# A written-out TensorE order that also names banks and sets, with residual loads moved and zero matmuls in more places

## The chip, the core and the metric

The kernel runs on one core of one Trainium2 chip. The metric is the time on the device in microseconds, from the core's start to its end. Times of several runs are given as their median and their spread; the profile is of one further execution.

## The reference

The input is x, 2048 tokens of 640 numbers. After a layer norm two branches read it, and their outputs are added to x. The first is attention with 32 query heads of 20 numbers that share one key head and one value head; the second is a feed-forward layer of width 1728 with SiLU. All inputs are bf16.

```python
xn = layernorm(x)                                   # 2048 x 640, eps 1e-5
q = (xn @ wq) -> 32 heads x 2048 x 20 ; k = xn @ wk ; v = xn @ wv   # k, v: 2048 x 20
p = softmax(q @ k.T * 20 ** -0.5)                    # per head, 2048 x 2048
attention = concat_heads(p @ v) @ wo
ffn = silu(xn @ w1) @ w2                             # w1: 640 x 1728, w2: 1728 x 640
return x + attention + ffn
```

## The kernel before

**One planner, five written orders.** The file is a program that plans the kernel. `Sched` and `Builder` keep a clock for every engine and a duration for every operation, place the operations one by one at planned times, and write each engine's instructions in the order so found, with semaphores between engines. On the chip there is no choice left: every engine, and SP's queue of DMAs too, works in its written order, and a planned time has no force except through the order that came out of it.

**Tiles.** The work of attention is 2048 blocks: 4 query chunks of 512 tokens, 32 heads, 16 key tiles of 128 tokens. Four heads that follow each other make a group; there are 32 groups of 64 blocks. A head has 20 numbers, so a head's queries and keys stand in a strip of 32 partitions, and four scores of different strips run beside each other in the array: block number modulo 4 is the strip, the "row". A score is one matmul (32x128 weights, 512 columns) into one PSUM bank of 128x512 (L1010, in the first part L1421).

**From scores to sums.** A score's exponential is made in one of two ways. ScalarE reads one, two or three neighbouring banks at once and writes the exponentials into slots of a ring of 30 (L1034, before that L1444). Or VectorE clamps the score to an integer whose bits are the exponential (L1050, L1461), and VectorE or GpSimd add two offsets to three such blocks at once (L1489, L1495), which gives three pieces that are summed with three scalings of the values. A "set of sums" is up to four matmuls side by side in four strips of 32 columns, one for each head of the group, which add one piece each to the group's sums in bank 7 (`UBANK`; L1092, in the first part L1336). When a group is complete, VectorE copies the sums out (L1539), a DMA on SP's queue transposes them (L1508), VectorE takes the reciprocal of the denominators (L1522) and GpSimd scales (L1527). Banks 0 to 6 serve scores and all other matmuls.

**Jobs.** The query projections of later chunks and the feed-forward and output products are cut into jobs of 4 to 19 steps. A step is four matmuls of 32 columns beside each other (L569), 512 or 320 wide. The last step of a job may instead be cut into four row pieces (L1188), which run beside scores in a strip that is free. A query job ends with a copy out of its bank (L1640) and small DMAs that bring heads to their strips (L1649). Residual rows of x are loaded again for the outputs (`load_res`, L1826), 8 loads of 160 KB for the last and the first chunk, and are read first by L1767.

**Modes.** Scores and row pieces use the array by rows; sums and job steps use it by columns. Going from one to the other costs PE time, which the planner knows as `SWITCH`.

**The order around the change.** The first part (normalisation, keys, values, first queries, first scores) is planned greedily by `step`; in its gaps `fill` puts zero matmuls (L1252), so that PE is not idle. When at least 64 blocks are scored and the first part's jobs are used up, `step` enters the string `ORDER`, one letter for each PE step:

- a and A: a score for ScalarE; the capital closes the group of banks that one exponential reads.
- d and D: a score for VectorE; the case tells which engine adds the first offset.
- p: a set of sums. j: a job step. k: a row piece of a job step.

In the kernel before, the letters say what comes next but not where: `run_banks` and `one_bank` choose banks by the planned times at which they come free, and `open_pv` takes for each head the first piece that is ready at the planned time. `tail` does what is left after the string.

**SP's queue.** SP takes the DMA that is ready first in planned time. The eight residual loads may not be placed before the planned time `RES_AT`:

```python
if op.name == "res":
    op.at = RES_AT
```

Of the kernel before, what the change touches and what calls it, by code (L numbers as in the profile page):

```python
# [14 lines left out]
P = 128  # L15
# [35 lines left out]
RES_AT = 62.0  # L51
# [33 lines left out]
    "aADDaAdppdaAppaAaAppppaADdDppaAdppaADjjdaAkppDaAkpjdaAkppjadkApjaAkppppaADDjpppDaAkjaADkpjpadkAjjjpa"  # L85
    "ADjpjaADppDaAdppDaAjjaADjjdaApjDaAppjjjaADjjpaAdppaADpjjpaADpjaAdjjDaAppDaADppaAdppdaAdppaAdjpaAdjja"
    "ADjjaAdpppjaADkpppaAdkjjdaAkpjdakApppaADjjjdaAjjjaADkjpdaAkpjdaAkjpdakAjjjjjAAdppDaApppDaAdpppaDAppD"
    "aAdjjaAppdadAjjjaDAppaAdjjpjdaApjjaAdpppDaAppDaADpjjaADpjaADpjaAdpjDaAjjjjpjaAdppaADjjjjjaADppAAdppp"
    "aAdppDaADjjjaADppaADpjjaAdpaAdppjjdaAjjpaAdpjdaAppDaADppaADjpjadAkjjpDaAkjjjjadAkjpjakADjjjdaAjjjjaD"
    "AkjjjDaAkjjjDaAkjjjDakApppaAdppDaAjpDaAkjjdaAkjpDaAkppDkaApppaDAppDDaAppdaAppDaApppdaAappDDAppdaAjjp"  # L90
    "aADkjjpaDAkjjjDaAkjpjdakAjjjjaDAppdaAppADaAppjjjADDAkjjjjaAdkjpdaAkjjjjaDAkjpDaAppdaApppadAdpppDaApp"
    "aDdApDaApppADAkppadAkjjaAdkjjpakADppdaAppaAdppDDAAppdaAjjjjpaADkjjjdAAkjpjaADkjjjjaAdkppDDAAppdaAjpj"
    "aADkjpjDaAkjjpjaAdkjpjdakAjpDaAjjjdaApppdaAdppDaAppaADppDaADppADAppjDaAkjpaADkpjjaADkppakAkjjjdaAkpj"
    "jdaAkjjjjaAdkjjjjaDAppaDAppDaADppDaApppadAppaADDppDaAppdaAkjjjjaAdkjjjjDaAkjjkAdAppjDaApjpDaApjpAAdp"
    "dAAdpjppaADjaADjjjaADppDAApjDaAjjaAdpjjpdaAppaADpppdaAppdaAdpppaDAppaADpDdaApjjaAdjjjadApaAdppppDaAD"
    "pjjaADpjaADpjjaADppaDAjjjdaAjpjpaAdjjjjjaDAppdaApppdaAdppaADjjaAdjpjjpaADaADpppjjaAdpjadApjjdaAjpjjd"
    "aApdaApppdaAdjjpaAdpaAdppppdaAjjjaAdDjjpaDApadApjjjDaAjpjaADpppDaAkpjDaAkjpjdaAkpdakAppjaAdpDadAppDa"
    "AjjpdaAjDaAjpjDadAppjaAppjaAddjjjadApppAADppDdaApjjpaAdjdaAjjpDaApjpaAdjjaAdpjjaAdppaADpppDDaApjjpaA"
    "dkjjjaAdkjjjdaAkjjjjaAkDjpdaAjjjjjDaApDdaApppaAdppDAAppDaADpppaAdpdAAdpjjaADpjaADpjaADjpdaAppDaAjpjj"
    "aADkjjjaAakjjjjAddkjjjkaAjjjDaAjjpaAdppaAddppdaApppaAdDppaAdppaAdppdaADpppaAdppaADDppaADpDaApjpaDAjj"  # L100
    "jdaAkjjjdaAkjjjjjaADkjjjDakAjjjDaAppdaAppjaAaAjjjjpaDAdppdaAppaADDpppADAppadAdppadApppadAappDADppDaA"
    "pjjjaADjjjaDAjpAAdkjjjjdaAkjjjjaAdkjjjDkaApppAaaAppaADpjpjjjjjDaDAjjjjjjAADkjjadAkppjdAAkjpjjAkADppD"
    "AAdppaAdppadDApppaDdAppdaAppDaAdppaAkppdaAkppDaAkjjDaAkjjpaADdppaAdpjjaADkjjjaADkjjjjaADkjpDaAkjpjDa"
    "AkjjjDaApjpdaAkppDakApjpaAdppakAppDDaAppDaApppDaAdpjaAjjjjaAaAjjjjjjjjjaADdjjppdaAjpDaAjpjDaAppdDaAp"
    "paADppjaADkjjjjaAdkjjpaAdkjpkdaAjpjjdaAkjpjDaAkjjjaAdkjpdaAkpppdaADppaAdppDaApdaADpppaADDppaAppaADDp"
    "pDaAjjaADpjaADjpjjaAdjjjjpaADaAjpppjDaAdjjjpaAdpaAdpppDaAdpppDaApdaADppaAdppDaApjjDaAjjaAdjpaADjppja"
    "AdjjpjpaADaAjjjppdadAjpjpaADpdaApjpjadAjpDaAjjdaAjpjjaAdjpjaDAppjpDaAjjDaAppjadADjpppaDAaAjjpjpdaAdj"
    "jpaADpaAdpppdaAdpjpadAjjadAjjadAppadAdppDaAjppaAdjdaAjjjaADdppaAjjjjAADdpjpjaAjjAADpjjaDAppaAdppdadA"
    "pppaDAppDaAppAAdDpjjaAdjaDAjppaDADjpppaAdaDAppjjaAdppaAdjjjpaAdjpaAkjppdaAkjjdaAkppdaAkjjjjaAkjjjjaA"
    "dkjjjaAdkjjjkdaAjjjjaAdppDdaApppDaAppdaADppaAdppdaAppdaADpppaADppDaAkjjjaAdkjjjadAjjjjakAjjjdaAdjjjj"  # L110
    "jaAdpkdaAppdaDAppadApppdaAdpjaAkpjadAkjDaAkpppDaAkpjdaAppaADdppDaAppdaAppDaAjppaDAjjjDaAkjpjDaAkpjjj"
    "aAdkjjjkdaAjppaADkppaADkjpjdaAkpjjdaAkppDaADppDaAjjjjDaAkppaAdkjjjdaAkpjpDakAppDaAkppDaAkppjDaAkppaA"
    "DkjppdaAkpjDaAkppDAAkjjpkdAAjjjppdAAkppAAkjpaAddjpppdakAjaAdpjdkaAjjjjjaADkjjpaAkjjjAADdjpjpjAAkdjjj"
    "daAppkaADjjppdaADppDaAppAADdppaADjjjjaADkjjjjaADkjjpaAdkjpDkaApjjjaAdpjdaAjjpjaAdppdaADppaAdppaADDpp"
    "aAdjjjjaADkjpjaADkpjDaAkpjjjkDaAjjDaAkpjjpDaAkppdaAkppaAdkpjpadAkppdaAkppaAdppDADkpkAaAjppADAdjjjpja"
    "ADkjjaAdkjjjjjaADkjjjdkaAjjjjaADppdaAdppaADppAAdpppaADaAdpjjjjaAdjppaAdppaADjpjjDaAjjpDaApdAApppddaA"
    "pppDaAdppAAdppAADpDaApjjjaADdpjjppaAdpDaApjjjaAdjjdaAjjpjDaAjjdaApjjjpdaAjjdaApjjjjdaApjDAppAdaAjjpj"
    "jjdaAdpjjjjjjDaAjjjjaAdpppDaAppddaAppAADppdaAdppDaApppAAdDppaADjppdaAjjaAdjjdaAjjpjDaAjppdaAjpdaAjpj"
    "jjjDaApppdaApDaADppAADpjjjjjaADkjdaAkjjjjjaAddjjpjjaADkjjDkaAppjaADppdaAdppDaAppaAdppDaADpppaADppaAD"
    "pjjaAdjjjdaAkjjdaAkjjjjDaAkjjjjdAkAjjjDaAppdaApjjpaAaAjjjjjjjjjDaAdjjjjjjaADkppdaAkppAADkppjdkaAppaA"  # L120
    "DppdaAappAddpppaAapppAaADpDdpppDaAdppaADjjjjaAdjjaADkppdaAkjjjDaAkjjjjkDaAjjpjDaAjjpDaAppdaADppaADpp"
    "AADppaAdapppADppAAdDpjjjaADkjjjaAdkjjaAdkjjjjjkaAAAjjjjpjpdadApppAdAdppaAdppDaADppaAdjjjjaAdkjjjjadA"
    "kjpjaDAkjjdakAppppaADkpaAdkpppDdAAkpjjppjAkADaADpjpjjpjjjpjjjpjDaAjjjpjjAADApjjjjdADAjpjjjpjjjpjjjaA"
    "ADaApjjjjjpjjjpjjjjpjjjjjppjjpjjpjjjpjjjpp"
)
Z_COST = 0
# [351 lines left out]
class Builder:  # L478
# [97 lines left out]
    def steps_init(self):  # L576
# [26 lines left out]
        self.jl = []  # L603
        self.tq = [[[] for _ in range(4)] for _ in range(self.NG)]
# [364 lines left out]
    def open_score(self, tok, now):  # L969
# [9 lines left out]
        if act and self.grp is None:  # L979
            n = 0  # L980
            for t in ORDER[self.at:]:
                n += t in "aA"
                if t == "A":
                    break
            r, run, bt = self.run_banks(n, now)
            if run is None:
                return INF
            first = min(run, key=lambda b: (bt[b] > now + 1e-9, b))
            if bt[first] > now + 1e-9:
                return bt[first]  # L990
            if self.blk_pos + n > NBLK:
                self.blk_pos = 0
            self.grp = {"banks": run, "todo": list(run), "b0": self.blk_pos, "at": nb}
            self.blk_pos += n
        if act:
            todo = self.grp["todo"]
            bt = {b: self.bank_at(b) for b in todo}
            b = min(todo, key=lambda b: (max(bt[b], now + 1e-9), b))
            if bt[b] > now + 1e-9:
                return bt[b]  # L1000
            todo.remove(b)
        else:
            r, b = self.one_bank(now)
            if r > now + 1e-9:
                return r
# [54 lines left out]
    def open_pv(self, now):  # L1060
# [7 lines left out]
        for q in self.tq[g]:  # L1068
            got, when = None, INF
            for it in q[:8]:  # L1070
                r = max(sc.ready(it), self.reads_ready([("vv", it.kt // 2)]))
                if r <= now + 1e-9:
                    got = it
                    break
# [3 lines left out]
            elif not (closed and len(q) < most):  # L1078
                return when
# [1205 lines left out]
```

## Time and profile before

| | |
|---|---|
| median of 3 runs | 682.20 us |
| the runs | 682.20, 682.48, 679.81 us |
| the profiled execution | 679.33 us |
| its span, first to last instruction | 677.2 us |
| mean granted TensorE clock | 0.995 |
| PE, ACT, DVE, POOL busy | 98%, 96%, 93%, 83% |
| score matmuls in the order, in the first part | 1977, 71 |

Busy time is the time in which an engine had at least one instruction in work; matmuls overlap, and their ends are modelled, so PE's share alone does not say how much of it is needed. In the timeline a row gives the start, the length, the engine, the line, the operation and its shapes, how many instructions were merged into it, and in brackets the idle time before it with what ended it. A mean length of one instruction contains its latency; the spacing of the starts is the price.

### The profile page before, as it was taken

To read this page: it belongs to the slowest core of one execution; us is meant where nothing else is said; L and a number is where in the kernel's file an instruction comes from. 1 tells how busy PE (TensorE), PEld (TensorE's weight loads), DVE (VectorE), ACT (ScalarE), POOL (GpSimd) and SP (SyncE) were. 2 spreads that over 40 slices of the span, in tenths; PEclk is the share of its full clock that TensorE was granted. 3 is DMA by queue.
4 is the path that set the end of the run, shared out by engine and by line. 5 is a ranking of instruction groups with operands and counts; after the bars stand their busy time and mean duration, and the time that the engine had idled before them with its cause. 6 is when DMAs were issued, how large, how long until landed. Compare 5 with 4: busy or idle time off the path is not lost.

```text
span 677.2 us, 22217 instructions
## 1 busy us (share of the span) xinstructions
PE 666.5 (98%) x9690; PEld 226.9 (34%) x9693; DVE 632.8 (93%) x1136; ACT 652.6 (96%) x798; POOL 561.6 (83%) x443
## 2 busy tenths in 40 slices
PE   9799999999999999999999999999999999999997
PEld 4332223323333333333333333333333333233335
DVE  7999899999999999999999999999999999998985
ACT  6999899999999999999999999999999999999983
POOL 4478888888887888888889888898878889989883
PEclk9899899999999999999999999999999999999999
DMA  7468300000013000020103000101014210000012
GB/s 208 97 196 247 114 15 10 10 18 10 17 17 56 10 10 10 17 37 17 30 17 70 20 10 10 26 16 31 10 30 54 31 29 10 9 3 20 19 35 67
DMA packets 53239, 28.14 MB, mean 42 GB/s; under 512 B 39094, under 2 KB 52502, under 8 KB 53142
## 3 DMA queue, kind: packets, MB, share of 16 engines
q1 hardware_dynamic: 52854, 26.40, 16.0%
q8 instruction: 76, 1.25, 0.8%
q10 hardware_dynamic: 288, 0.33, 0.1%
q14 instruction: 21, 0.17, 0.1%
HBM read 11.44 MB, written 2.62 MB: 21 GB/s over the span
## 4 chain that ended last, share of the span: by engine, by line
PE 94%; DVE 4%; DMA 1%; issue 0%; another core or an unknown queue 0%; POOL 0%; ACT 0%; ACTq 0%
PE psall L1092 34%; PE psall L1010 29%; PE psall L569 28%; DVE sbt L2009 1%; PE psall L1421 1%; PE psall L1336 1%; DVE sbt L1461 1%; PE psall L2180 1%; PE psall L1188 0%; DMA sbt<-in_A_x_dram 0%; DVE sbt L1050 0%; PE psall L1670 0%; DMA sbt<-sbt 0%; PE psall L1252 0%; DVE sbt L2172 0%
## 5 line engine op out<-in xcount | busy, mean ns | idle before, releaser
L1034 ACT ACTIVATE sbt<-psall 128x1024 bf16<-128x1024 f32 (+2 forms) x686 | 598.7, 1030 | 5.7 <-PE psall L1010 5.0
L1495 POOL TENSOR_TENSOR sbt<-sbt 128x768 int32<-128x768 int32 (+1 forms) x374 | 527.7, 1438 | 85.8 <-DVE sbt L1489 81.9
L1050 DVE TENSOR_SCALAR sbt<-psall 128x512 int16<-128x512 f32 x710 | 458.6, 683 | 26.8 <-PE psall L1010 19.0
L1092 PE MATMUL psall<-sbt 128*32 128x512 bf16 x3438 | 281.7, 384 | 0.1
L1010 PE MATMUL psall<-sbt 32*128 32x512 bf16 x1977 | 253.4, 386 | 1.2 <-DVE sbt L1050 1.0
L569 PE MATMUL psall<-sbt 128*32 128x320 bf16 (+1 forms) x3667 | 230.4, 333 | 0.3 <-DVE sbt L1050 0.2
L1010 PEld LDWEIGHTS psall<-sbt 32*128 32x128 bf16 x1977 | 67.8, 91 | 232.6 <-ACT sbt L1034 93.6
L569 PEld LDWEIGHTS psall<-sbt 128*32 128x32 bf16 x3667 | 81.9, 96 | 83.3 <-issue 48.9
L1092 PEld LDWEIGHTS psall<-sbt 128*32 128x32 bf16 x3438 | 69.6, 95 | 99.0 <-issue 76.0
L1489 DVE TENSOR_SCALAR sbt<-sbt 128x1536 int16<-128x1536 int16 (+2 forms) x128 | 71.0, 571 | 0.4
L1188 PE MATMUL psall<-sbt 32*128 32x320 bf16 (+1 forms) x196 | 63.3, 324 | 0.0
L1689 DVE SCALAR_TENSOR_TENSOR sbt<-sbt,psall 128x512 bf16<-128x512 bf16 (+1 forms) x56 | 38.1, 680 | 0.5 <-ACT sbt L1681 0.3
L1681 ACT ACTIVATE sbt<-psall 128x512 bf16<-128x512 f32 x54 | 37.5, 695 | 0.0
L1444 ACT ACTIVATE sbt<-psall 128x1024 bf16<-128x1024 f32 (+2 forms) x27 | 24.2, 985 | 3.0 <-PE psall L1421 2.7
L1527 POOL TENSOR_TENSOR sbt<-sbt 128x320 bf16<-128x320 bf16 x31 | 22.6, 728 | 2.9 <-DVE sbt L1489 2.5
L1539 DVE CAST sbt<-psall 128x512 bf16<-128x512 f32 x31 | 21.1, 682 | 0.6 <-PE psall L1092 0.5
L1188 PEld LDWEIGHTS psall<-sbt 32*128 32x128 bf16 x196 | 17.7, 91 | 3.4 <-issue 1.9
L2035 POOL TENSOR_SCALAR sbt<-sbt 128x640 bf16<-128x640 bf16 x7 | 6.1, 875 | 15.2 <-DVE sbt L2039 10.7
L1252 PE MATMUL psall<-sbt 128*128 128x512 bf16 (+6 forms) x54 | 14.5, 409 | 1.7 <-DVE sbt L1943 1.2
L1787 DVE SCALAR_TENSOR_TENSOR sbt<-psall,sbt 128x320 bf16<-128x320 f32 x28 | 13.3, 483 | 2.4 <-PE psall L569 1.1
L1461 DVE TENSOR_SCALAR sbt<-psall 128x512 int16<-128x512 f32 x20 | 13.2, 686 | 1.0 <-PE psall L1421 0.8
L1640 DVE TENSOR_SCALAR sbt<-psall 128x512 bf16<-128x512 f32 (+1 forms) x19 | 13.0, 683 | 0.5 <-PE psall L569 0.3
(85 smaller groups left out, 122.7 us busy)
## 6 DMA issues: line engine op xcount, KB each, us to landing
sbt<-in_A_x_dram SPq DMA_DIRECT2D x31, 160.0 KB, 3.4
out_dram<-sbt SPq DMA_DIRECT2D x15, 160.0 KB, 1.8
sbt<-in_B_w_dram SPq DMA_DIRECT2D x5, 432.0 KB, 5.3
sbt<-sbt SPq DMA_DIRECT2D x105, 20.0 KB
sbt<-in_B_w_dram SPq DMA_DIRECT2D x13, 160.0 KB, 3.1
sbt<-sbt SPq DMA_DIRECT2D x1, 1024.0 KB, 6.3
sbt<-sbt SPq DMA_TRANSPOSE x58, 2.5
sbt<-in_A_wo_dram SPq DMA_DIRECT2D x5, 160.0 KB, 3.1
```

The costliest lines, as they stand in the source:

```text
L569: ins = pe.matmul(self.bk(b, 0, n, j, j + SLOT), w[:, j:j + SLOT], x, start=start, stop=stop, tile_position=(0, j), skip_group_check=True)
L1010: return pe.matmul(self.bk(b), self.kT[row:row + SLOT, kt * P:(kt + 1) * P], self.qT[row:row + SLOT, g % 8, (g // 8) % 2, :], start=True, ...
L1034: return a.activation(self.E[:, b0 * QW:(b0 + n) * QW], self.ps[:, b1 * BANK:(b1 + n) * BANK], AF.Exp, scale=ACT_SCALE, bias=ACT_BIAS)
L1050: return v.tensor_scalar(self.Z[:, zs, zp * QW:(zp + 1) * QW], self.bk(b), 0.0, ZMAX, ALU.max, ALU.min)
L1092: ins = pe.matmul(self.bk(UBANK, 0, QW, r, r + SLOT), self.v[:, it.w, it.kt, :], it.x(), start=f, stop=False, tile_position=(0, r), skip_g ...
L1188: return pe.matmul(self.bk(b, 0, n), w[r0:r0 + SLOT, :], x[r0:r0 + SLOT, :], start=first, stop=last, tile_position=(r0, 0), skip_group_che ...
L1444: return a.activation(self.E[:, (b0 + lo) * QW:(b0 + lo + m) * QW], self.ps[:, b * BANK:(b + m) * BANK], AF.Exp, scale=ACT_SCALE, bias=ACT ...
L1489: sc.new("dve", td, lambda v, k=k: v.tensor_scalar(self.Y[:, zs, k, 0:w], self.Z[:, zs, 0:w], float(PH[k + 1][0]), None, ALU.add), zk, yk, ...
L1495: sc.new("pool", tp, lambda v, k=k, cb=cb: v.tensor_tensor(self.Y[:, zs, k, 0:w].bitcast(I32), self.Z[:, zs, 0:w].bitcast(I32), cb, ALU.ad ...
L1527: op = sc.new(eng, 0.75 if eng == "pool" else t_dve_ps(16 * DH), lambda v: v.tensor_tensor(dst, ut[:, :, :, 0:DH], rb, ALU.mult), [key, (" ...
L1681: sc.new("act", t_act(QW), lambda a: a.activation(t, src, AF.Tanh, scale=0.5), [("B", b)], [("tb", tp)], prio=X_PRIO, name=f"th{c}_{fk}")
L1689: sc.new("dve", t_dve_ps(QW), lambda v, r0=r0, r1=r1, ht=ht: v.scalar_tensor_tensor(out=ht[r0:r1, :], in0=t[r0:r1, :], scalar=1.0, in1=src ...
```

## The change

Four things are changed.

1. `RES_AT` goes from 62 to 96, so the eight residual loads get a later place in SP's queue.
2. `fill` may, before the order is entered, also put a zero matmul onto a bank that holds a score which its reader has not begun to read (`unread`). Such a matmul adds zero to what is there (`start=False`), and the readers get a dependence on it.
3. `ORDER` is another string, and two strings stand beside it: `BANKS` has a digit for every letter that takes a bank, and `SETS` has four signs for every p, one for each head, that name the key tile and the piece (a sign's place in `ABC` is key tile times three plus piece; "-" is none). `open_score`, `open_pv` and `job_open` take these and wait for them, where they chose by planned time.
4. What follows from it: the order is entered with 67 blocks scored in place of 71, since its scores begin there.

| letters | before | after |
|---|---|---|
| scores (a, A, d, D) | 1977 | 1981 |
| closed groups for ScalarE (A) | 686 | 684 |
| of two banks, one bank, three banks | 579, 106, 1 | 586, 97, 1 |
| p, with places left empty | 874, 58 | 868, 40 |
| j, k | 895, 196 | 894, 200 |
| runs of score letters and k | 617 | 614 |

The core of the diff, with the strings cut to their last lines:

```diff
-RES_AT = 62.0
+RES_AT = 96.0
...
-    "ADaApjjjjjpjjjpjjjjpjjjjjppjjpjjpjjjpjjjpp"
+    "aADdaAdppppaAapAddpppdaADaAAppADdpadAppaADpDaAkjjjdaAkpjaAdkppdaAkppjpaAkjpdaADppjaADkppaAdkjpdkaAjj"
...
...
+    "jjjjjpjjjjjAAAAjjjjjjjpjjjjpjpppjjpjjjjjjjj"
 )
+BANKS = (
...
+    "...........1236......5....4........5...6..."
+)
+SETS = (
...
+    "BCF5IFI8LILFOLOIRORLHREBUUUOMJGRXVXSaXaVNKHUPPSXQQTTdWdWgagajdjdegbgfjcj"
+)
+ABC = "0123456789ABCDEFGHIJKLMNOPQRSTUVWXYZabcdefghijkl"
...
+        sets = iter(SETS[i:i + 4] for i in range(0, len(SETS), 4))
+        self.sets = [next(sets) if t == "p" else None for t in ORDER]
...
-            r, run, bt = self.run_banks(n, now)
...
+            todo = [int(b) for b, t in zip(BANKS[self.at:], ORDER[self.at:]) if t in "aA"][:n]
+            run = list(range(min(todo), min(todo) + n))
...
-            b = min(todo, key=lambda b: (max(bt[b], now + 1e-9), b))
...
+            b = int(BANKS[self.at])
+            r = self.bank_at(b)
...
-        for q in self.tq[g]:
-            got, when = None, INF
-            for it in q[:8]:
...
+        for i, c in enumerate(self.sets[self.at]):
+            if c != "-":
+                it = next((it for it in self.tq[g][i] if it.kt * 3 + it.w == ABC.index(c)), None)
+                if it is None:
+                    return INF
...
+    def unread(self, now, dur):
...
+            w, rd = sc.lastw.get(("B", b)), sc.readers[("B", b)]
+            if w is None or w.eng != "pe" or w.name[0] != "S" or w.end is None or not rd:
+                continue
+            if any(d.start is not None or d.eng not in ("act", "dve") for d in rd):
+                continue
...
+            c = self.unread(now, n / 2400.0 + self.switch(mode)) if self.at < 0 and (self.cur_job is not None or r > now + 1e-9) else None
+            if c is not None:
+                b, ukey = c[0], None
...
-                return pe.matmul(self.bk(b, 0, n), self.zero[:, 0:P], self.zero[:, 0:n], start=True, stop=True)
+                return pe.matmul(self.bk(b, 0, n), self.zero[:, 0:P], self.zero[:, 0:n], start=c is None, stop=c is None,
+                                 skip_group_check=c is not None)
...
+        if mode == "M" and not onto and not self.u_open and c is not None:
+            for d in c[1]:
+                d.deps.add(op)
```

More of the change, by code (lines that the diff above doesn't have):

```diff
@@ L90 @@
[L90 to L99, printed above, removed]
@@ L1065, in open_pv @@
         closed = self.g_seen[g] == GB and not self.g_late[g]
[L1066 removed]
         items = []
[L1068 to L1079 removed]
+        for i, c in enumerate(self.sets[self.at]):
[3 more added lines that the diff above has]
+                    return INF
+                r = max(sc.ready(it), self.reads_ready([("vv", it.kt // 2)]))
+                if r > now + 1e-9:
+                    return r
+                items.append(it)
         if not items:
@@ L1121, in job_open @@
             return r
-        r, b = self.one_bank(now)
+        if self.at < len(ORDER):
+            b = int(BANKS[self.at])
+            r = self.bank_map().get(b, INF)
+        else:
+            r, b = self.one_bank(now)
         if r > now + 1e-9:
@@ L1209, in busy_share @@
         return tot / WIN
+    def unread(self, now, dur):
+        sc = self.sc
+        best = (now + dur + LAT["pe"] + 0.1, None)
+        for b in range(8):
+            w, rd = sc.lastw.get(("B", b)), sc.readers[("B", b)]
[3 more added lines that the diff above has]
+                continue
+            at = INF
+            for d in rd:
+                t = max(now, sc.t[d.eng]) + sum(x.dur for x in sc.pend[d.eng]
+                                                if x.name[:1] in "pe" and (x.prio, x.seq) < (d.prio, d.seq))
+                at = min(at, t)
+            if at > best[0]:
+                best = (at, (b, list(rd)))
+        return best[1]
     def fill(self, now, until):
```

168 lines of the change are left out of this document (121 added, 47 removed).

## The prediction

> **What bounds the kernel now.** The page comes first: the span, the engines' shares, the slices, the chain that ended last.
>
> ```profile
> span 677.2 us, 22217 instructions
> PE 666.5 (98%) x9690; PEld 226.9 (34%) x9693; DVE 632.8 (93%) x1136; ACT 652.6 (96%) x798; POOL 561.6 (83%) x443
> PE   9799999999999999999999999999999999999997
> PEclk9899899999999999999999999999999999999999
> PE 94%; DVE 4%; DMA 1%; issue 0%; another core or an unknown queue 0%; POOL 0%; ACT 0%; ACTq 0%
> ```
>
> Three engines are above 90%, but the chain runs through PE for 94% of the span. The reader should see two other things: PE's second slice is short, and the granted clock dips in slices 2 and 5. A busy share cannot tell a balanced engine from the one that decides, so the next view is PE's timeline in the middle of the kernel.
>
> ```profile
> 351.70 0.59 PE L569 MATMUL psall<-sbt 128*32 128x320 bf16 x12
> 352.22 0.39 PE L1010 MATMUL psall<-sbt 32*128 32x512 bf16 x3
> 352.55 0.40 PE L1092 MATMUL psall<-sbt 128*32 128x512 bf16 x4
> 352.77 0.31 PE L569 MATMUL psall<-sbt 128*32 128x320 bf16 x4
> 352.91 0.39 PE L1092 MATMUL psall<-sbt 128*32 128x512 bf16 x4
> 353.23 0.39 PE L1010 MATMUL psall<-sbt 32*128 32x512 bf16 x3
> ```
>
> Starts give prices. A set of sums costs 0.22 (352.55 to 352.77), a 320-wide job step 0.14 (352.77 to 352.91). A run of scores costs 0.32 to 0.33 (352.22 to 352.55): one 0.22 step and about 0.105 for the change of mode; the way back costs the same (352.91 to 353.23, one set and the change). A pair of changes is thus 0.21. The windows say how full PE is, at the end of the first part and in the middle:
>
> ```profile
> 36.00:45.50 9.50, 9.43 (x139) 3.84 (x136) 8.74 (x17) 8.24 (x11) 6.58 (x5) 1.00 0.84 321
> 100.00:300.00 200.00, 199.97 (x2877) 63.96 (x2880) 194.08 (x338) 199.99 (x241) 169.76 (x127) 1.00 0.09 17
> ```
>
> The columns are the stretch, its length, then PE, weight loads, DVE, ACT and POOL busy, the clock, the DMA share and GB/s. PE idles 0.07 us in 9.5 and 0.03 us in 200. So this part can be shortened only by fewer steps and changes of mode, and lengthened by waits; time is lost visibly only before 84 us.
>
> ```profile
> 18.62:22.04 3.42, 2.24 (x34) 1.25 (x33) 3.42 (x13) 3.42 (x6) 1.44 (x3) 1.00 0.51 114
> 22.04:25.45 3.41, 1.92 (x33) 1.37 (x34) 3.10 (x15) 3.41 (x5) 0.87 (x1) 1.00 0.21 48
> 25.45:28.86 3.41, 3.29 (x13) 0.74 (x12) 2.68 (x6) 2.41 (x3) 0.57 (x1) 0.50 0.43 96
> 76.65:80.06 3.41, 2.22 (x29) 0.58 (x23) 1.97 (x5) 2.82 (x4) 2.19 (x3) 1.00 0.23 53
> 80.06:83.48 3.42, 3.42 (x33) 0.59 (x25) 2.53 (x5) 1.98 (x2) 2.10 (x2) 0.50 0.10 25
> ```
>
> Twice PE runs 3.41 us at half clock, each time right after a stretch of that length in which it was 56% and 65% busy.
>
> **The residual loads.** Eight loads move. Where they stand now, on SP's queue:
>
> ```profile
> 63.86 6.13 SPq L1826 DMA_DIRECT2D sbt<-in_A_x_dram  x8
> 70.52 5.21 SPq L1649 DMA_DIRECT2D sbt<-sbt  x7
> 75.78 1.27 SPq L1508 DMA_TRANSPOSE sbt<-sbt  x1
> ```
> ```profile
> 63.35 0.69 DVE L1640 TENSOR_SCALAR sbt<-psall 128x512 bf16<-128x512 f32 x1
> 68.66 0.68 DVE L1539 CAST sbt<-psall 128x512 bf16<-128x512 f32 x1
> 78.25 0.25 DVE L1522 RECIPROCAL sbt<-sbt 128x16 f32<-128x16 bf16 x1 [1.44 <-DMA sbt<-sbt]
> ```
>
> The seven query copies could go at 64.04 (63.35 + 0.69), and the transpose of the second group's sums at 69.34. The eight loads hold the queue until 69.99, the copies then until 75.73, so the transpose starts 6.4 late. DVE, which works in a written order, stands 1.44 before the reciprocal, and the clamps behind it free score banks late:
>
> ```profile
> 77.73 0.39 PE L1010 MATMUL psall<-sbt 32*128 32x512 bf16 x2
> 79.10 0.39 PE L1010 MATMUL psall<-sbt 32*128 32x512 bf16 x1 [0.98 <-DVE sbt L1050]
> 79.69 0.40 PE L569 MATMUL psall<-sbt 128*32 128x512 bf16 x4 [0.20 <-DVE sbt L1050]
> 83.39 0.41 PE L1010 MATMUL psall<-sbt 32*128 32x512 bf16 x3
> ```
>
> From 77.73 to 83.39 PE does three score runs and three runs of two wide steps: 3 x 0.32 + 3 x (2 x 0.22 + 0.105) = 2.60, and takes 5.66. Of the 3.06 lost, 1.37 + 0.27 = 1.64 is waiting (77.73 to 79.69, less one run), and 1.42 is the half clock behind it. With the loads gone the copies end at 64.04 + 5.21 = 69.25, before the cast does; the transpose is on time, and both losses go: **-3.06**. What is late next? The loads' new place:
>
> ```profile
> 95.17 1.22 SPq L1508 DMA_TRANSPOSE sbt<-sbt  x1
> ```
> ```profile
> 114.47 1.19 SPq L1508 DMA_TRANSPOSE sbt<-sbt  x1
> ```
> ```profile
> 131.91 0.48 DVE L1767 SCALAR_TENSOR_TENSOR sbt<-psall,sbt 128x320 bf16<-128x320 f32 x1
> ```
>
> SP issues nothing between 96.39 and 114.47, and the loads need 6.13. The constant is in the planner's time, where 62 became 63.86 in the trace; the transpose at 95.17 would itself come 3 earlier. So 96 falls behind it, into the gap. The first reader of a residual is at 131.91, some 30 us later. Cost there: nothing, covered by that gap; without it, the same 3.06 again.
>
> **The zero matmuls.** They add work to PE's gaps in the first part, on banks that hold scores not yet read, and each named reader waits for them. Existing ones are the nearest row:
>
> ```profile
> L1252 PE MATMUL psall<-sbt 128*128 128x512 bf16 (+6 forms) x54 | 14.5, 409 | 1.7 <-DVE sbt L1943 1.2 <-DVE sbt L2207 0.5
> ```
>
> That is 0.27 us each. The two stretches from 18.62 have 1.18 and 1.49 us free, and ACT is 100% busy with scores waiting for it, so such banks exist. If they keep the clock up, the stretch from 25.45 gets back at most half of PE's 3.29, 1.65 us; part of it is DVE's own chain. If they come in the way of an exponential, five of them cost 1.4. I take **-1.2**, nearer to the upper end because the same clock row cost 1.42 at 80 us. [...]
>
> **The new order.** Scores in it: 1977 and 1981, so the first part does 71 blocks before and 67 after. PE is full there (9.43 of 9.50), and four blocks are one or two visits of 0.32 to 0.43: **-0.6**, bounds 0 and -2. Counting both strings up to the last score, a score's row being its number modulo four and a k piece taking the row that is free first: sets 863 to 862 (-0.22), wide job steps 348 to 347 (-0.22), narrow ones 520 to 525 (+0.70), score runs 617 to 614 (-0.63), steps inside score runs +1.3 wide ones (+0.29). Together **-0.1**, although four more blocks are in it. Behind the last score:
>
> ```profile
> 662.97:673.46 10.49, 9.35 (x220) 6.28 (x220) 1.00 0.17 34
> ```
> ```profile
> 662.97:673.46 10.49, 2.82 (x26) 0.93 (x26) 1.00 0.17 34
> ```
>
> These are the job steps (220 matmuls, 55 steps) and the sums (26) after the last score. The strings leave 27 and 22 job steps there, so 50; and 11 sets with 18 places empty (26 matmuls) become 6 full ones (24). Five steps of 0.14 and half a set: **-0.8**. The last eight job steps stand behind the last set and cover its eviction, which may save a few tenths more.
>
> Fixed banks and sets add no instruction. Their price is a wait where the named bank or block is late: below, in the second rival; in the sum nothing, because the same seven banks serve about the same number of scores.
>
> **Sum.** -3.06 - 1.2 - 0.6 - 0.1 - 0.8 = -5.8. The profiled execution took 679.33 (span 677.2 and 2.1 around it), the median run 682.20, the runs 679.81 to 682.48. Half-clock stretches of 1.4 us more or fewer would make such a spread, and I cannot tell how many a run has; I start halfway, at 680.8, and forecast **675.0**.
>
> **The rivals.** *The clock does not answer to the fills or the stall.* Then 1.64 + 0.6 + 0.1 + 0.8 = 3.14 is gained: 677.6. For it: the stretch from 18.62 was only 66% busy and was followed by full clock. Against: both halvings follow the emptiest stretches. Chance 0.12.
>
> *Fixed banks make PE wait.* Before, the planner takes the bank that is free first by its own times; now a score waits for its named bank, and everything behind it on PE.
>
> ```profile
> PEld psall L1010 <- ACT sbt L1034: 93.6, 248, 0.4
> PEld psall L1010 <- issue: 52.3, 148, 0.8
> ```
>
> A load that waits for ACT idles 0.377 on average, one that waits for nothing 0.353. If this difference of 0.024 came on top in each of 614 score runs, 14.7 us: 689.7, slower. It decides from 0.017 a run, (685.6 - 675.0) / 614. For it: every score run starts just as a bank comes free. Against: the present order was written out beforehand too, and PE hardly waits. Chance 0.08.
>
> *ScalarE becomes the bound.*
>
> ```profile
> L1034 ACT ACTIVATE sbt<-psall 128x1024 bf16<-128x1024 f32 x579 | 552.3, 1097 | 5.0 <-PE psall L1010 4.3
> L1034 ACT ACTIVATE sbt<-psall 128x512 bf16<-128x512 f32 x106 | 59.8, 661 | 0.7 <-PE psall L1010 0.7
> ```
>
> By the strings, double exponentials go from 579 to 586 and single ones from 106 to 97: 7 x 0.954 - 9 x 0.564 = +1.6. ACT is 199.99 of 200 busy. If it set the pace, -0.1 becomes +1.6: 676.7. Against: PE starts with no delay beyond its own prices. Chance 0.08.
>
> *The loads do not fall into the gap* but ahead of another transpose; the 3.06 is lost there instead: 678.1. Chance 0.06.
>
> **How the numbers follow.** The forecast has 0.66. A measurement of this kernel can tell about 0.5%, 3.4 us: faster ends at 678.8, slower begins at 685.6. Most of the forecast and of the first, third and fourth rivals lies under 678.8, together 0.78; the rest of them, with the high start (682.20) and small gains, is 0.14; the second rival gives 0.08. Low end: the low start 679.33, with 2.0 for the entry, 1.65 for the clock and 1.0 in the tail, is 671.5, and the tail's cover takes it to 670.5. High end: 682.20 with the waiting alone removed is about 680.6, and some new bank waits make it 681.5.
>
> **What would show it.** SP's rows: the query copies near 64, the transpose right behind the cast, the loads after the third transpose. DVE's reciprocal without the 1.44; no PE step longer than 0.6 near 78, and clock 1.00 from 60 to 100. Clock 1.00 from 22 to 29, and more zero matmuls. The first L1010 before 45; 24 matmuls of L1092 and 200 of L569 after the last score. Wrong it is if PE's share between 100 and 650 falls below 99%, or a half-clock stretch appears at another place.

## The result and the profile after

The changed kernel takes 676.12 us (median of 9 runs, 675.63 to 676.91). The kernel before, run beside it, takes 681.39 (9 runs, 676.93 to 682.48). The ratio is 0.9932, 95% interval 0.9913 to 0.9950. The profiled execution took 676.14, with a span of 674.0, where that of before took 679.33 with 677.2. One of 21 runs of the kernel before in a later group took 1399.4 us and is left out of all medians and ratios.

The page of the changed kernel, in its lines on the span, the engines, the slices and the chain that ended last, and its group of zero matmuls:

```profile
span 674.0 us, 22209 instructions
PE 664.9 (99%) x9693; PEld 224.9 (33%) x9696; DVE 629.2 (93%) x1133; ACT 652.9 (97%) x794; POOL 558.0 (83%) x441
PE   8899999999999999999999999999999999999997
PEclk9999999999999999999999999999999999999999
PE 65%; ACT 29%; DVE 5%; DMA 0%; issue 0%; POOL 0%; ACTq 0%
...
L1353 PE MATMUL psall<-sbt 128*128 128x512 bf16 (+6 forms) x63 | 16.5, 392 | 1.4 <-DVE sbt L2048 1.2
```

The granted clock has lost its two dips, and there are 63 zero matmuls of L1353 (L1252 before) in place of 54. The chain no longer runs through PE alone: ScalarE carries 29% of it. Line numbers are 76 to 105 higher than before: scores are L1090, sums L1168, job steps L649, exponentials L1114, clamps L1130, transposes L1613, the reciprocal L1627, query copies L1754, residual loads L1931.

SP's queue in the timeline, then two rows of DVE's:

```profile
63.35 6.56 SPq L1754 DMA_DIRECT2D sbt<-sbt  x7
70.36 1.99 SPq L1613 DMA_TRANSPOSE sbt<-sbt  x1
...
92.55 1.22 SPq L1613 DMA_TRANSPOSE sbt<-sbt  x1
93.81 3.91 SPq L1931 DMA_DIRECT2D sbt<-in_A_x_dram  x8
```
```profile
68.89 0.68 DVE L1644 CAST sbt<-psall 128x512 bf16<-128x512 f32 x1
73.79 0.24 DVE L1627 RECIPROCAL sbt<-sbt 128x16 f32<-128x16 bf16 x1
```

The copies start at 63.35, where the loads used to start; the transpose follows 0.79 behind the cast's end; the loads stand behind the third transpose; and the reciprocal has no wait in brackets.

The windows (stretch, length, busy PE, weight loads, DVE, ACT, POOL, clock, DMA share, GB/s):

```profile
18.55:21.96 3.41, 3.25 (x38) 1.65 (x36) 3.41 (x12) 3.41 (x6) 1.59 (x3) 1.00 0.57 129
21.96:25.37 3.41, 2.30 (x35) 1.34 (x35) 3.10 (x16) 3.41 (x5) 0.87 (x1) 1.00 0.21 48
25.37:28.79 3.42, 3.17 (x22) 1.05 (x20) 3.42 (x9) 3.12 (x4) 0.57 (x1) 1.00 0.43 96
20.93:24.34 3.41, 2.49 (x32) 1.10 (x31) 3.10 (x16) 3.41 (x4) 0.08 (x1) 1.00 0.43 96
76.57:79.99 3.42, 3.42 (x49) 1.01 (x45) 3.42 (x7) 3.42 (x5) 2.56 (x3) 1.00 0.10 25
100.00:300.00 200.00, 199.97 (x2882) 62.62 (x2878) 195.27 (x340) 200.00 (x241) 168.63 (x126) 1.00 0.10 19
```

The clock is 1.00 in all of them. The first three rows lie where the slow stretches of before lay. The clock's own stretches of 3.41 us, counted from the first full clock (3.86 us in this execution, 4.97 in that of before), lie elsewhere here: the sixth begins at 20.93, and PE is 73% busy in it; before, 56% was followed by half clock. The stretch from 76.57 is full. The last row still has 0.03 us of PE idle in 200, and ScalarE has none.

The windows from the last score to PE's end, job steps first, then sums:

```profile
660.10:670.01 9.91, 8.45 (x204) 4.88 (x200) 1.00 0.10 35
660.10:670.01 9.91, 1.95 (x24) 0.64 (x24) 1.00 0.10 35
```

200 weight loads of job steps (four of the 204 matmuls belong to the step that was still running) and 24 sums, as counted from the strings: 9.91 us, where before took 10.49.

The same points in the two traces show where 3.2 us of span went:

| point | before | after | after less before |
|---|---|---|---|
| first score of the order | 45.51 | 44.32 | -1.19 |
| score of block 128 | 63.24 | 63.13 | -0.11 |
| score of block 200 | 88.64 | 86.22 | -2.42 |
| last score | 662.97 | 660.10 | -2.87 |
| PE's end | 673.46 | 670.01 | -3.45 |
| end of the span | 677.2 | 674.0 | -3.2 |

The entry comes earlier, but with four blocks fewer scored; at block 128, where both have scored the same number, almost nothing of it is left. The gain comes between blocks 128 and 200; 570 us of attention and jobs behind that give 0.45, the tail 0.58.

### The profile page after: what moved, and what is told of

It is laid out like the page before. It is cut to its first block, busy times and chain, and to the rows that moved or that the text cites. A ratio compares the mean times of both kernels' runs of the same rounds, so it can differ in the third digit from the quotient of the medians.

```text
span 674.0 us, 22209 instructions
## 1 busy us (share of the span) xinstructions
PE 664.9 (99%) x9693; PEld 224.9 (33%) x9696; DVE 629.2 (93%) x1133; ACT 652.9 (97%) x794; POOL 558.0 (83%) x441
## 4 chain that ended last, share of the span: by engine, by line
PE 65%; ACT 29%; DVE 5%; DMA 0%; issue 0%; POOL 0%; ACTq 0%
ACT sbt L1114 28%; PE psall L1168 23%; PE psall L1090 20%; PE psall L649 19%; ACT sbt L1786 1%; DVE sbt L2114 1%; DVE sbt L1566 1%; PE psall L1441 1%; DVE sbt L1130 1%; DMA sbt<-in_A_x_dram 0%; PE psall L1268 0%; PE psall L1526 0%; PE psall L1775 0%; PE psall L2285 0%; DVE sbt L2291 0%
## 5 line engine op out<-in xcount | busy, mean ns | idle before, releaser
L1114 ACT ACTIVATE sbt<-psall 128x1024 bf16<-128x1024 f32 (+1 forms) x684 | 601.1, 1039 | 2.5 <-PE psall L1090 2.3
L1130 DVE TENSOR_SCALAR sbt<-psall 128x512 int16<-128x512 f32 x709 | 456.3, 681 | 23.8 <-PE psall L1090 15.0
L1168 PE MATMUL psall<-sbt 128*32 128x512 bf16 x3432 | 281.6, 384 | 0.2 <-DVE sbt L1644 0.2
L1090 PE MATMUL psall<-sbt 32*128 32x512 bf16 x1981 | 252.6, 384 | 0.7 <-DVE sbt L1566 0.2
L649 PE MATMUL psall<-sbt 128*32 128x320 bf16 (+1 forms) x3663 | 227.7, 332 | 0.0
L1090 PEld LDWEIGHTS psall<-sbt 32*128 32x128 bf16 x1981 | 67.3, 91 | 228.1 <-ACT sbt L1114 91.0
L649 PEld LDWEIGHTS psall<-sbt 128*32 128x32 bf16 x3663 | 79.3, 95 | 82.4 <-issue 46.7
L1168 PEld LDWEIGHTS psall<-sbt 128*32 128x32 bf16 x3432 | 69.1, 94 | 101.6 <-issue 75.7
L1268 PE MATMUL psall<-sbt 32*128 32x320 bf16 (+1 forms) x200 | 64.7, 325 | 0.0
L1549 ACT ACTIVATE sbt<-psall 128x1024 bf16<-128x1024 f32 (+2 forms) x25 | 23.0, 1023 | 2.8 <-PE psall L1526 2.8
L1353 PE MATMUL psall<-sbt 128*128 128x512 bf16 (+6 forms) x63 | 16.5, 392 | 1.4 <-DVE sbt L2048 1.2
L2114 DVE BATCH_NORM_STATS2 sbt<-sbt 128x6 f32<-128x320 bf16 x24 | 10.5, 468 | 2.7 <-DMA sbt<-in_A_x_dram 2.7
```

The lines of the kernel that those rows point to most:

```text
L649: ins = pe.matmul(self.bk(b, 0, n, j, j + SLOT), w[:, j:j + SLOT], x, start=start, stop=stop, tile_position=(0, j), skip_group_check=True)
L1090: return pe.matmul(self.bk(b), self.kT[row:row + SLOT, kt * P:(kt + 1) * P], self.qT[row:row + SLOT, g % 8, (g // 8) % 2, :], start=True, ...
L1114: return a.activation(self.E[:, b0 * QW:(b0 + n) * QW], self.ps[:, b1 * BANK:(b1 + n) * BANK], AF.Exp, scale=ACT_SCALE, bias=ACT_BIAS)
L1130: return v.tensor_scalar(self.Z[:, zs, zp * QW:(zp + 1) * QW], self.bk(b), 0.0, ZMAX, ALU.max, ALU.min)
L1168: ins = pe.matmul(self.bk(UBANK, 0, QW, r, r + SLOT), self.v[:, it.w, it.kt, :], it.x(), start=f, stop=False, tile_position=(0, r), skip_g ...
L1268: return pe.matmul(self.bk(b, 0, n), w[r0:r0 + SLOT, :], x[r0:r0 + SLOT, :], start=first, stop=last, tile_position=(r0, 0), skip_group_che ...
```

## The experiments

**Late loads alone.**

```diff
 # kernel before
-RES_AT = 62.0
+RES_AT = 96.0
```

> The kernel before with the one constant changed, residual loads at planned 96. Theory (the loads held up the second group's transpose on SP's queue): the transpose starts right behind the cast near 69.4 us, the reciprocal no longer waits 1.44 us for it, PE has no step above 0.6 us near 78, and the clock stays 1.00 there; the profiled span falls by 3.06 us, from 677.2 to about 674.1, and the median by 0.4 to 0.6%. A half-clock stretch near 25 us may still be there. Rival (the new order brings the gain): less than 1 us. Rival (the clock does not answer to the stall): 1.64 us, and a half-clock stretch stays in most executions.

Measured: 676.24 (675.05 to 676.38, 6 runs) beside 679.18 for the kernel before; ratio 0.9951 [0.9935, 0.9967]. SP's and DVE's rows in the timeline:

```profile
64.41 6.23 SPq L1649 DMA_DIRECT2D sbt<-sbt  x7
71.08 2.10 SPq L1508 DMA_TRANSPOSE sbt<-sbt  x1
74.39 0.25 DVE L1522 RECIPROCAL sbt<-sbt 128x16 f32<-128x16 bf16 x1 [0.57 <-DMA sbt<-sbt]
```

One constant gives nearly as much as the whole change. It also changes DVE's written order: the reciprocal stands five instructions earlier than in the kernel before. The seven copies took 5.21 where they stood before and 6.23 here, and the transpose 2.10 where it took 1.27; 0.57 us of the reciprocal's wait stays. Run again in another group of runs the same kernel took 676.47 (675.84 to 677.32, 11 runs), ratio 0.9943 [0.9926, 0.9959]:

> Late loads alone a second time, for the comparison with the changed kernel on one chip: the median within 0.4 us of the first time (676.24), about 3 us below the kernel before.

**Loads behind the second transpose, at 69.** The edit is that of the first experiment with 69.0.

> The kernel before with residual loads at planned 69: behind the second group's transpose, but 27 us of planned time earlier than 96. Theory (only the place in the queue matters): the same as with 96 within 0.5 us, about 674.1 us of span, the query copies that follow are late by some 6 us without anyone waiting. Rival (what counts is DMA traffic or the loads' landing in this stretch, or the late copies): the gain is half or less, and a wait on the query copies' DMAs or a stall between 75 and 90 us shows.

Measured: 676.57 (674.81 to 676.86, 6 runs), ratio 0.9953 [0.9936, 0.9970]. The loads went out right behind the transpose, from 73.08 to 76.96, and cost no more there than at 96, although the reciprocal waits 0.82. Between these two places there is no difference to be seen: both are behind that transpose.

**The new order alone.**

```diff
 # changed kernel
-RES_AT = 96.0
+RES_AT = 62.0
```

> The changed kernel with residual loads back at planned 62. Theory: the wait for the second group's transpose is back, near 78 us; 1.6 us more than the changed kernel where the clock holds, 3.1 us more where it halves behind it, so 677.7 to 679.2 us, and a wider spread. Rival (the new order does not need the late loads, since sets and banks are laid around them): within 0.5 us of the changed kernel.

Measured: 676.11 (675.52 to 676.93, 6 runs), ratio 0.9953 [0.9938, 0.9969]. The new order, with the loads back at their old place, gives as much as late loads alone. The timeline of SP and DVE:

```profile
64.81 5.76 SPq L1931 DMA_DIRECT2D sbt<-in_A_x_dram  x8
...
75.05 1.26 SPq L1613 DMA_TRANSPOSE sbt<-sbt  x1
...
77.53 0.25 DVE L1627 RECIPROCAL sbt<-sbt 128x16 f32<-128x16 bf16 x1 [0.43 <-DMA sbt<-sbt]
```

The loads still delay the transpose to 75.05, but the reciprocal waits 0.43 where it waited 1.44, PE idles once, for 0.29 us, near 78, and the clock holds (1.00 from 73.00 to 83.20). With the loads back at 62 the planner put the reciprocal five instructions later than in the changed kernel. So a late transpose need not cost the time; what counts is how DVE's written order stands to it. The next experiment but one tests that alone.

**Both parts in one group of runs.** The changed kernel again, beside the repeat of late loads:

> The changed kernel itself, beside the late loads alone on the same chip. If order and zero matmuls have a worth of their own: 0.8 to 1.5 us less than late loads alone, as matmul time from the first score to PE's end has it. If what they save at the entry of the order is given back where the order begins, and the rest lies in the spread: within 0.5 us of late loads alone.

Measured: 675.83 (674.96 to 676.17, 6 runs), ratio 0.9935 [0.9911, 0.9960]. On the same chip, late loads alone took 676.47: between medians the rest of the change adds about 0.6 us to them, no more. The parts are two ways to remove one loss, and their gains do not add.

**The order with the loads at their true price.** The loads stay at 62 in the kernel before; the planner is only told how long SP takes to issue one (6.13 / 8 = 0.77 us in the trace; it planned with 0.46).

```diff
 # kernel before, load_res, each of the 8 loads
+            op.dur = 0.77
```

> The kernel before, loads still at planned 62 and still ahead of the copies and the transpose, but the planner is told 0.77 us for each of the eight loads, as the trace has it, in place of 0.46. Nothing else is told. Only the order follows: the second group's reciprocal stands five instructions later in VectorE's order. Theory (the lateness of the transpose costs nothing by itself; what costs is that VectorE's order was written for an earlier landing, so that the clamps behind the reciprocal wait): the transpose still starts near 75.8 us, the reciprocal waits less than 0.5 us, no half-clock stretch near 80 us, and the median is that of late loads alone within 0.6 us, about 3 us below the kernel before. Rival (a late transpose costs by itself, through the scaling and what follows): half of the 3 us or less.

Measured: 676.42 (676.06 to 676.92, 6 runs) beside 680.62, ratio 0.9942 [0.9922, 0.9961].

```profile
64.58 5.78 SPq L1826 DMA_DIRECT2D sbt<-in_A_x_dram  x8
70.88 5.22 SPq L1649 DMA_DIRECT2D sbt<-sbt  x7
76.14 1.26 SPq L1508 DMA_TRANSPOSE sbt<-sbt  x1
...
79.03 0.25 DVE L1522 RECIPROCAL sbt<-sbt 128x16 f32<-128x16 bf16 x1
```
```profile
76.65:80.06 3.41, 3.41 (x45) 1.00 (x44) 3.41 (x8) 3.41 (x5) 2.37 (x3) 1.00 0.24 58
```

SP's queue is that of before but for one small copy that moves by two places, and the transpose starts at 76.14, later than the 75.78 of before. Yet there is no wait: the reciprocal now stands five instructions later in DVE's order, clamps go ahead of it, and PE is full. Little else differs in the program: two neighbours on GpSimd change places, and seven matmuls differ. This settles the cause: a DVE order planned with a price that was too low for the loads.

**Padding the standstill.** The wait stays, and four matmuls of zeros, added into the sums' bank, run where PE stood still.

```diff
 # kernel before, behind the score of block 175
+PAD_AT = 175
...
+            for _ in range(4 if nb == PAD_AT else 0):
+                pe.matmul(self.bk(UBANK, 0, QW, 0, 32), self.zero[:, 0:32], self.zero[:, 0:QW], start=False, stop=False,
+                          tile_position=(0, 0), skip_group_check=True)
```

> The kernel before with four zero matmuls, added into the open sums, put between the second and the third score of the run that stands still near 78 us (block 175); nothing is taken away. Theory (the half-clock stretch near 80 us is the answer to the standstill of PE, and costs 1.4 us of its own): the four matmuls take some 1.1 us of the 1.37 us wait and cost nothing, the waits on the transpose stay, the clock stays 1.00 after 80 us, and executions that had one half-clock stretch more come out about 1.4 us shorter: the median falls by 1 to 1.5 us against the kernel before, to about halfway between it and the kernel with late loads. Rival (the clock does not answer to gaps of this length): same time as before or up to 0.3 us more, and the half-clock stretch stays.

Measured: 678.33 (677.65 to 680.99, 12 runs) beside 680.87; the interval of the ratio, 0.9982 [0.9962, 1.0002], just touches 1, so the times alone do not show a gain. The clocks do show something: none of the 12 executions had a mean clock under 0.995, where 9 of the 20 of before in the same group had 0.992. The trace says more; timeline, then windows:

```profile
78.06 1.04 PE L1014 MATMUL psall<-sbt 128*32 128x512 bf16 x4
78.95 0.26 DVE L1527 RECIPROCAL sbt<-sbt 128x16 f32<-128x16 bf16 x1 [2.13 <-DMA sbt<-sbt]
79.80 0.39 PE L1011 MATMUL psall<-sbt 32*128 32x512 bf16 x1 [0.71 <-DVE sbt L1055]
```
```profile
76.65:80.06 3.41, 2.70 (x27) 0.77 (x19) 1.28 (x4) 2.83 (x4) 2.19 (x3) 1.00 0.23 54
80.06:83.48 3.42, 3.22 (x42) 0.92 (x45) 3.42 (x7) 2.11 (x3) 1.40 (x1) 1.00 0.11 28
```

In this execution the reciprocal waited longer than before, 2.13 against 1.44, and the third score came at 79.80, 0.70 later. Still block 200 was scored at 87.95, 0.69 earlier than before: the stretch from 76.65 was 79% busy, not 65%, and the next one kept full clock. The half clock was thus an answer to the standstill, worth about 1.4 in this pair of profiles (0.70 + 0.69), as the prediction put it. No idle gap of PE before reached 1.5 us (the longest after the first matmul was 1.49), and four matmuls of 1.04 us together, put into the standstill, kept the clock. At this place 65% busy lost the clock and 79% kept it; the last section has full clock behind 57% and 59% too.

**Thin zero matmuls.** The nine zero matmuls on unread banks write 32 columns in place of up to 512, so they keep their place and do a fraction of the work.

```diff
 # changed kernel, fill
-                return pe.matmul(self.bk(b, 0, n), self.zero[:, 0:P], self.zero[:, 0:n], ...
+                m = n if c is None else 32
+                return pe.matmul(self.bk(b, 0, m), self.zero[:, 0:P], self.zero[:, 0:m], ...
```

> The changed kernel, where the zero matmuls on unread score banks are written with 32 columns and everything else, order and waits too, stays. Theory (those matmuls keep the clock up in the first part): PE is less than 70% busy in one or two of the 3.41 us stretches between 18 and 29 us, a half-clock stretch is back near 25 us in part of the executions, and these take up to 1.65 us longer; the spread of the runs grows. Rival (the clock there does not answer to so few matmuls, or the first part's end is not set by PE): same median as the changed kernel within 0.4 us, and no half-clock stretch.

Measured: 676.50 (675.77 to 676.92, 6 runs), ratio 0.9957 [0.9943, 0.9972]: 0.38 and 0.67 us above the two medians of the full ones, 676.12 and 675.83. Three of the six executions had a mean clock of 0.997, about what one stretch of 3.41 us at half clock takes from it (an estimate: 0.5 x 3.41 / 675 = 0.0025), and three of 1.0; the profiled one is of the latter, so where the others lost it is not shown. The new zero matmuls were not run with the old string: the first part that has them ends with 67 blocks, and the old string's 1977 would leave four of the 2048 over. What they are worth alone is therefore not measured.

**Banks and sets by planned time.** The changed kernel with its letters, but with banks, or banks and sets, chosen as before.

```diff
 # changed kernel, open_score; open_pv and job_open likewise
-            todo = [int(b) for b, t in zip(BANKS[self.at:], ORDER[self.at:]) if t in "aA"][:n]
-            run = list(range(min(todo), min(todo) + n))
...
+            r, run, bt = self.run_banks(n, now)
...
-            b = int(BANKS[self.at])
-            r = self.bank_map().get(b, INF)
...
+            r, b = self.one_bank(now)
```

Both by planned time:

> The changed kernel with its new letters, but banks and blocks chosen by planned time as in the kernel before; late loads and zero matmuls stay. Theory (the letters were laid out together with the named banks and blocks; without them a letter meets a bank or piece that is late, and everything behind it on PE waits): slower than the changed kernel by more than 3 us, with PE's idle time spread over the order and waits on ACT and DVE. Rival (names add nothing, letters decide): within 1 us of the changed kernel.

Banks alone by planned time, sets named:

> The changed kernel with its letters and named sets, banks chosen by planned time. (With named banks and sets chosen by planned time the program comes out the same as the changed kernel, so the names of the sets are not run apart.) Theory (the named banks are what the letters need): as slow as with both free, 690 us within 3. Rival (the sets matter): near 676.

Measured: 690.82 (690.20 to 691.03, 5 runs), ratio 1.0157 [1.0129, 1.0184], and 693.43 (693.19 to 693.75, 4 runs), ratio 1.0193 [1.0164, 1.0222]. One window over the middle, for both by planned time, the changed kernel, and banks by planned time:

```profile
100.00:650.00 550.00, 544.69 (x7913) 174.28 (x7909) 517.27 (x886) 541.42 (x638) 462.82 (x344) 1.00 0.09 21
```
```profile
100.00:650.00 550.00, 549.88 (x8155) 178.14 (x8147) 528.04 (x906) 549.19 (x654) 473.64 (x352) 1.00 0.10 21
```
```profile
100.00:650.00 550.00, 542.19 (x7879) 173.00 (x7876) 515.34 (x880) 539.50 (x635) 462.17 (x343) 1.00 0.10 22
```

PE idles 5.3 and 7.8 us where the changed kernel idles 0.1, and ScalarE 8.6 and 10.5 where it idles 0.8. In the same 550 us the kernel with both by planned time gets 242 fewer matmuls done than the changed kernel, which at 8155 in 549.88 us are 16.3 us of its work; so some 11 us more lie in time that counts as busy, and these runs do not split them. The view of waits shows where one of them grows (us in total, times, longest):

```profile
PEld psall L1092 <- DVE sbt L1132: 54.0, 138, 1.1
```
```profile
PEld psall L1090 <- DVE sbt L1130: 47.9, 121, 0.4
```

The first row is the kernel with both by planned time, the second the changed one: the longest wait of a score for a clamp goes from 0.4 to 1.1. The new letters are good only with the banks that they were written with. Named banks with sets by planned time was not run. Planned so, the program is not quite that of the changed kernel, against what the expectation says: 180 of its 9696 matmuls differ, nearly all of them sums that take another piece. What the string `SETS` is worth is therefore not shown; with the banks free, naming the sets did not help (693.43 against 690.82).

## Why the prediction was right or wrong

**Where it started, and the total.** The start of 680.8 was 0.6 under the median now measured, 681.39, and the sum of -5.8 became -5.3 between medians. The two profiles differ by only 3.2. The profiled execution of before had two half-clock stretches, and others had more. Sorted by the mean granted clock, 31 runs of the kernel before in the first two groups of experiments have medians of 677.84 (clock 0.9985 and up, 5 runs), 679.69 (0.995 up to there, 16) and 681.61 (about 0.992, 10). One half-clock stretch of 3.41 us is 0.0025 of the mean clock (0.5 x 3.41 / 677). All 15 runs of the changed kernel have a clock of 0.999 or 1.0 and lie between 674.96 and 676.91. So the step that guessed half-clock stretches behind the spread held: against the executions of before with full clock the change gains about 1.7 (677.84 to 676.12), and the rest of the gain between medians, some 3.6 (681.39 to 677.84), goes with the lost clock. That 675.0 came within 1.1 of 676.12 is in part luck. The terms were read from the profiled execution, and there -5.8 became -3.2, so they were 2.6 too large; the start, set 1.5 above that execution, made up for more than half of it.

**Residual loads, -3.06.** Place, wait and clock were as forecast. From block 128 to block 200, in before, in the changed kernel, and in the kernel with the true price:

```profile
63.24:88.64 25.40, 24.21 (x303) 6.44 (x299) 21.70 (x38) 23.19 (x28) 20.70 (x16) 0.93 0.42 136
```
```profile
63.13:86.22 23.09, 23.09 (x312) 7.08 (x308) 21.83 (x39) 23.02 (x29) 21.50 (x17) 1.00 0.27 82
```
```profile
62.69:85.26 22.57, 22.57 (x301) 6.47 (x299) 21.52 (x38) 22.57 (x28) 20.65 (x16) 1.00 0.50 155
```

With the old letters and no wait left the stretch is 2.83 shorter, close to the 3.06. The changed kernel gains 2.31; PE is full there too, but its letters have three more job steps in this stretch (27 against 24). One duration was wrong: the copies were taken to need 5.21 at their new place, and took 6.56, right behind the issue of five 160 KB weight loads (to 62.29). A word was wrong too: the transpose "late" was read as the cause, and with the true price in the planner it is as late and costs nothing. The 3.06 was DVE's order against that queue. That is also why the term does not add to the order's: the new order alone removes most of the same wait.

**Zero matmuls, -1.2.** The clock did as forecast, but the time was not kept. There are 63 zero matmuls, and the clock is full to 29 us. All 15 executions of the changed kernel keep it (0.999 or 1.0), where 9 of 23 with loads at 96 or 69 alone had a mean clock of 0.997. The first profile of late loads alone still has the slow stretch:

```profile
22.61:26.02 3.41, 1.79 (x31) 1.22 (x29) 3.17 (x13) 3.36 (x5) 0.87 (x1) 1.00 0.10 22
26.02:29.44 3.42, 3.06 (x14) 0.76 (x16) 2.36 (x6) 1.94 (x2) 1.10 (x2) 0.50 0.58 131
```

Yet those nine executions took 676.17 to 676.86 (median 676.33), and the fourteen with a mean clock of 0.999 or 1.0 took 674.81 to 677.32 (median 676.42). The mean hides a second loss: it counts recorded stretches at half clock, not the time before the first full clock (it is 1.0 in the second profile of late loads, where full clock came at 6.75 us), and that time differs between executions of one kernel (5.54 and 6.75 us in the two profiles of late loads). PE is slower in it: before, the weight loads of zero matmuls start 0.42 or 0.43 us apart up to 4.99, and the next six take 1.18 together. The twelve profiles tell the two apart (us from the start):

| first part | first full clock | half clock near 25 | first score of the order |
|---|---|---|---|
| old: before, padded, loads at 96 (first time), loads at 69 | 4.77 to 5.54 | yes | 45.36 to 45.78 |
| old: loads at 96 (second time), true price | 6.75, 6.65 | no | 44.99, 44.95 |
| new: changed (both), banks or banks and sets by planned time | 3.86 to 5.39 | no | 44.18 to 44.32 |
| new: loads at 62; thin zero matmuls | 6.88; 7.14 | no | 44.91; 45.23 |

Where full clock came early, the new first part ends 1.0 to 1.6 us sooner than the old one, which then lost a stretch. Where it came late, the old one lost none, and the new one ends no sooner. The prediction knew of the first case only. And the new first part ends with four blocks fewer, so these differences hold both this term and the next; no run parts them.

**Entry, -0.6.** This step failed: most of what the entry saves is given back right behind it, in part by waits that the sum had at nothing. The table's -1.19 at the first score holds this term and the last one, and -0.11 of it is left at block 128. From the first score to block 128, before and changed:

```profile
45.51:63.24 17.73, 17.35 (x232) 5.17 (x230) 15.94 (x28) 17.60 (x21) 15.35 (x12) 1.00 0.54 157
```
```profile
44.32:63.13 18.81, 18.00 (x233) 5.54 (x230) 17.28 (x31) 18.63 (x23) 15.46 (x13) 1.00 0.58 172
```

The old letters take 17.73 or 17.74 here in all six profiles, the new ones 18.80 or 18.81 in five of six, whether the entry comes at 44.2 or at 45.2. Of the 1.08 more, 0.65 is busy time, in which 61 scores are made in place of 57, and 0.43 is idle time of PE (0.81 against 0.38). Some of the waits, in PE's timeline of the changed kernel:

```profile
44.32 0.39 PE L1090 MATMUL psall<-sbt 32*128 32x512 bf16 x3
44.92 0.70 PE L1090 MATMUL psall<-sbt 32*128 32x512 bf16 x4 [0.21 <-DVE sbt L1566]
49.58 0.62 PE L1168 MATMUL psall<-sbt 128*32 128x512 bf16 x8 [0.21 <-DVE sbt L1644]
51.97 0.39 PE L1090 MATMUL psall<-sbt 32*128 32x512 bf16 x3 [0.21 <-DVE sbt L1130]
```

The four scores are in the order's count, and that count makes up for them only later in the string. The waits are in no term: the step took PE to be full on both sides of the entry, and quoted a row for the near side only.

**Order to the last score, -0.1.** The count was of the whole string. From the first to the last score, in the changed kernel's second profile and in the kernel with the true price:

```profile
44.22:659.80 615.58, 614.64 (x9075) 200.21 (x9072) 585.49 (x1005) 613.08 (x735) 532.60 (x396) 1.00 0.13 31
```
```profile
44.95:659.93 614.98, 614.53 (x9055) 201.02 (x9052) 585.70 (x1003) 611.55 (x738) 534.22 (x396) 1.00 0.13 31
```

In PE's busy time the count was nearly right: 0.1 more where 0.1 less was forecast. But PE idles 0.94 against 0.45, so the new string is 0.6 longer, not 0.1 shorter, most of it by the waits behind the entry. From block 200 to the last score the profile gains 0.45 against before. **Tail, -0.8:** the counts were right to the matmul, and 0.58 came. The time from PE's end to the end of the span was 3.1 to 4.0 us in the twelve profiles, so a few tenths from the cover of the last eviction can't be seen.

**Rivals.** "The clock does not answer" was wrong at both places: padding kept the clock behind 80 us (1.00 from 80.06 to 83.48), and where full clock came early, four profiles of four with the old first part had half clock near 25 and none of four with the new one and its full zero matmuls; with thin zero matmuls three of six executions had a mean clock of 0.997. "Fixed banks make PE wait" had it the wrong way round for these letters: with banks and sets by planned time they take 690.82, with names 675.83. The old letters reach 676.24 with late loads and no names, so the names are what the new letters need, and no gain in themselves. "ScalarE becomes the bound" is not decided: it is 200.00 of 200 busy, but was 199.99 before, and it now carries 29% of the chain. That the loads fall ahead of another transpose did not occur.

## What to carry to other kernels

In a schedule written out beforehand, a wrong price can show as a wait on another engine (here 0.46 planned for a load that took 0.77, and 1.44 us of waiting on DVE): before you move the late instruction, look for the first planned duration that the trace contradicts, and try the true price. Two edits that remove the same wait do not add, so run each alone before you sum them. Compare two orders at a point where both have done the same work: an entry 1.19 us earlier was worth 0.11 there. And a mean clock may leave out part of the lost clock (it was 1.0 where full clock came at 6.75 us), so look at when full clock first came before you compare executions by it.

## What the runs showed of the hardware

The clock changed on a grid of 3.41 us. In before it is full from 4.97 to 25.45 us (20.48, six times 3.41), half for 3.41, full for 51.20 (fifteen times) and half for 3.41 again; in the changed kernel it is full from 3.86 to 672.88 (669.01, 196 times) and half behind that. In stretches on this grid PE's busy share does not decide alone. Half clock followed stretches that were 53% (late loads), 56% (before, loads at 69, padded) and 65% busy (before, from 76.65). But full clock followed 57% (true price) and 59% (late loads, second profile), and 64% to 66% in eight other stretches. The 57% row:

```profile
23.71:27.13 3.42, 1.95 (x17) 1.05 (x18) 3.28 (x12) 3.00 (x5) 0.87 (x1) 1.00 0.07 17
27.13:30.54 3.41, 2.76 (x19) 1.05 (x19) 3.41 (x7) 3.41 (x4) 1.79 (x2) 1.00 0.57 127
```

What else decides stays open. No idle gap of PE in the twelve profiles, between 6 and 660 us, was longer than 1.51 us.

The first full clock came between 3.86 and 7.14 us after the start in the twelve profiles, at 3.86 in the changed kernel and 4.97 before: a spread of 3.28, just under one stretch. The first matmul came at 1.18 or 1.19 in all of them.

SP's issue of one small SBUF copy took 0.74 us (5.21 for 7) in before's place, and 0.84, 0.89 and 0.94 (5.85, 6.23 and 6.56 for 7) when moved up beside the end of the weight loads. The eight residual loads took 0.77 us each in before's place (6.13 for 8), right behind the weight loads, and 0.49 (3.91) behind the third transpose.
